# State products interleaved with the softmax denominators, and a list schedule built again from traced durations

## The chip, the cores and the metric

The kernel runs on one core of one Trainium2 chip. The metric is the device time of one execution in microseconds (us); smaller is better. A core has five engines with a queue each: TensorE (PE in the profile; its weight loads are the row PEld), VectorE (DVE), ScalarE (ACT), GpSimd (POOL) and SyncE (SP), which here issues every DMA. The engines meet only through semaphores.

## The reference

One pre-norm transformer block over 2048 tokens of width 1024, in bf16. The attention has 32 heads of width 32 and works on four segments `s` of 512 tokens; each head carries a state `M` (32x32) and a sum of keys `z` from segment to segment. Then a gated feed-forward block of width 3584 (FFN). Cut to what matters:

```python
phi = lambda t: jnp.where(t > 0, t + 1.0, jnp.exp(t))
...
for s in range(N):                       # 4 segments, 32 heads
    p = softmax(einsum('bhqd,bhkd->bhqk', qs, ks) * scale + mask)
    a_dot = einsum('bhqk,bhkd->bhqd', p, vs)
    a_mem = einsum('bhld,bhde->bhle', phi(qs), M) / (einsum('bhld,bhd->bhl', phi(qs), z)[..., None] + 1e-06)
    outs.append(g * a_mem + (1.0 - g) * a_dot)
    M = M + einsum('bhld,bhle->bhde', phi(ks), vs)
    z = z + einsum('bhld->bhd', phi(ks))
...
h = x + attention(layernorm(x)) @ wo
h2 = h + (silu(layernorm(h) @ w1) * (layernorm(h) @ w3)) @ w2
```

## The kernel before, in words

**Recording and planning.** The program is not written in the order in which it runs. Methods of `Kernel` record operations in a `Graph`: each operation has an engine (or a choice of two), a cost in ns, the regions that it reads and writes, a class and a sequence number. `Graph.schedule` then plays a list scheduler: at each moment an engine takes the ready operation with the lowest class and number. What comes out is one fixed order for each engine, which `Graph.emit` writes down with semaphore waits. Costs are the planner's alone: they decide the order and, between DVE, ACT and POOL, who does a copy; they are not in the program. DMAs are operations of SP; their landing is planned from `DMA_RATE`, `DMA_FIX` and a byte count that `scale` corrects. Each call of `stage()` begins a numbered unit, and the table `SHIFT` gives a unit an offset of its sequence number and of its class: it is the knob with which the order was searched. `LATER` moves single units of PE's final order by hand.

**Work on TensorE.** Three kinds of matmuls share it. *Full* ones (128x128 weights, up to 512 columns, line L759): projections, output projection, FFN. *Score* bursts (L1113, 32-row tiles): four or eight matmuls that fill PSUM banks 0 to 3, which ACT empties with one exponential over 128x2048 (L1127); there are ten for each half of the heads of each segment, 80 in all. *Column* bursts (128x32 tiles): for every segment and half, four numerators (L1206, `et` times `v`), the denominators (L1206, `et` and partial sums against `ones32`, one piece for each of the four heads `j`) and, for `s` below 3, the state products (L1041): 64 matmuls of 33 columns that add up `phi(k)^T [v, 1]` in PSUM bank 7. Besides, six *retrieval* bursts (L1328). Full matmuls have banks 5, 6 and 7 while attention lasts, and all eight afterwards.

**Order around the change.** `finish` records numerators 0 to 2, the denominators, numerator 3 and then, by `memory`, the 64 state products as one operation of PE. The denominators already hold both banks (`Both(gd, gm)`: 4 and 7). Behind them DVE transposes the denominators (L1237), takes reciprocals, and adds the state products to `Macc` (L1056, L1057), which gives bank 7 back. The FFN's first half is started while attention still runs, to fill PE between score bursts. A full matmul waits until its bank has been emptied by a copy (DVE L783 or ACT L782) or, in the FFN, by tanh (ACT L1401) and two products (DVE L1404, L1409). Layer norm of later tiles (DVE L886 on `xs`) waits for loads from DRAM.

Of the kernel before, what the change touches and what calls it, by code (L numbers as in the profile page):

```python
# [30 lines left out]
    0: (-18, 0), 3: (-173, 0), 4: (-182, 0), 5: (1074, 0), 6: (1041, 1), 7: (-959, -1),  # L31
    8: (-283, 1), 9: (1560, 1), 10: (-14, 0), 11: (1, 0), 12: (51, -1), 13: (-257, 0),
    14: (-1703, 0), 15: (2952, 0), 16: (-2912, 0), 18: (-87, -1), 19: (3455, 1), 20: (-401, -1),
    21: (22, 0), 22: (2924, -1), 23: (-669, 0), 24: (-328, -1), 26: (-261, -1), 27: (11, -1),
    28: (-153, 0), 29: (-317, 0), 31: (1524, -1), 32: (211, 0), 33: (-1, 0), 34: (2, 0),
    35: (-15, 0), 38: (118, 1), 39: (2057, 0), 40: (223, 0), 41: (2279, -1), 42: (914, 1),
    43: (-1135, 1), 44: (2665, 1), 45: (3218, 1), 47: (1997, 1), 48: (664, -1), 49: (1928, -1),
    50: (-2800, -1), 51: (7, 0), 52: (-1130, 0), 53: (116, 0), 54: (669, 0), 55: (1018, 0),
    56: (2, 0), 57: (-289, 1), 58: (4, 0), 59: (731, 0), 60: (-304, 0), 61: (-436, 0),
    62: (64, 1), 63: (-3, 0), 64: (-63, 0), 65: (-50, 0), 66: (-174, 0), 67: (-937, 0),  # L40
    68: (808, 0), 69: (1512, -1), 70: (28, 0), 71: (-58, 1), 72: (1441, 1), 73: (-75, 1),
    74: (2141, 0), 75: (778, 1), 76: (-752, 1), 77: (90, 1), 78: (-21, 0), 79: (151, 0),
    80: (1343, 0), 81: (-1130, 0), 83: (160, 0), 84: (687, 0), 85: (-676, 0), 86: (312, 0),
    87: (-266, 0), 88: (-263, 0), 89: (-1189, -1), 90: (-164, 0), 91: (680, 1), 92: (-1801, 0),
    93: (1499, 0), 94: (3153, 0), 95: (-261, 0), 96: (0, -1), 97: (-11, 0), 98: (2, 0),
    99: (944, 0), 100: (-54, 0), 101: (1016, 0), 102: (-842, 0), 103: (147, 0), 104: (-1191, 0),
    106: (-47, 0), 107: (121, 1), 108: (-1142, 0), 109: (-1295, -1), 111: (699, 0),
    112: (-365, -1), 113: (-594, 0), 115: (28, 0), 116: (2452, -1), 117: (-8, 0), 118: (676, 0),
    119: (54, 0), 120: (-1449, -1), 121: (235, 0), 122: (-9, -1), 123: (-13, 1), 124: (45, 0),
    125: (-1279, 1), 127: (-283, -1), 129: (555, 0), 130: (1438, -1), 132: (617, 1),  # L50
    133: (81, 0), 134: (-2285, -1), 135: (-179, 0), 136: (3199, 1), 137: (389, 0),
    138: (920, 0), 139: (146, 1), 140: (687, 1), 141: (27, 0), 142: (-619, 1), 143: (1934, 1),
    144: (-922, 0), 145: (415, -1), 146: (-312, 0), 147: (-26, 0), 148: (-870, 0),
    149: (2501, 1), 150: (1682, 0), 151: (-28, 0), 152: (609, 1), 153: (611, 0), 154: (-302, 0),
    156: (0, 1), 157: (-185, 1), 158: (391, 0), 159: (-373, 0), 160: (-610, 0), 161: (-1748, 0),
    162: (-133, 0), 163: (-4056, 1), 164: (1073, 1), 166: (-202, 0), 168: (-3204, -1),
    169: (-2075, -1), 170: (2581, -1), 171: (-39, 1), 172: (-122, 1), 173: (-18, 1),
    174: (-37, 0), 175: (34, 0), 176: (1853, 1), 177: (-140, 0), 178: (-301, 0), 179: (204, 0),
    181: (165, 0), 182: (-13, 0), 183: (-7, 0), 184: (687, -1), 185: (-271, 0), 186: (-861, 1),
    187: (-616, 1), 188: (355, -1), 189: (-1449, 1), 190: (1132, 0), 191: (114, 0),  # L60
    192: (-22, 0), 193: (-464, 0), 194: (-2, 0), 195: (294, 0), 196: (18, 0), 197: (-2089, 0),
    199: (-2443, 0), 200: (248, -1), 201: (1, 0), 203: (210, 1), 204: (-1070, 0), 206: (-70, 0),
    207: (1441, 0), 208: (525, 0), 209: (839, 0), 210: (10, 0), 211: (-262, 0), 212: (894, -1),
    213: (203, 1), 214: (-359, 1), 215: (-2, 0), 216: (696, -1), 217: (-735, 0), 218: (-51, 0),
    219: (4750, 0), 220: (-465, -1), 221: (-23, 0), 222: (-196, 1), 223: (399, 0),
    224: (-1932, 1), 225: (-192, 0), 226: (-134, 0), 227: (-1542, 1), 229: (153, 1),
    230: (-676, 1), 231: (-73, 0), 232: (618, 1), 234: (-465, 0), 235: (0, -1), 237: (222, -1),
    238: (609, 0), 239: (1282, 0), 241: (-183, 1), 242: (845, 1), 243: (811, -1),
    244: (1681, -1), 246: (6, 1), 248: (-2423, -1), 249: (11, 0), 250: (21, 0), 251: (-2902, 1),
    252: (-599, 1), 253: (927, 0), 255: (308, -1), 256: (4, -1), 257: (-382, 0), 258: (30, 0),  # L70
    259: (-35, 0), 260: (-73, -1), 261: (-386, 0), 262: (-58, 1), 263: (-1713, 0),
    264: (-165, 0), 265: (-369, 1), 266: (-12, 0), 267: (808, -1), 268: (1356, 0),
    269: (-538, 0), 270: (576, -1), 272: (27, 0), 273: (609, 0), 275: (-27, 0), 277: (0, -1),
    279: (-4, 0), 280: (-3, 0), 281: (176, 0), 282: (-28, -1), 284: (-175, -1),
    285: (-1255, -1), 286: (-196, 0), 287: (308, 0), 288: (1028, 0), 289: (-18, 0),
    290: (-217, -1), 291: (628, 0), 292: (21, 0), 293: (11, 0), 294: (1042, 0), 295: (6, 0),
    296: (150, -1), 297: (222, 0), 298: (1329, 0), 299: (-799, 0), 300: (-3, 0), 301: (303, -1),
    302: (-473, -1), 303: (2419, -1), 304: (528, 0), 305: (-99, 0), 306: (2531, -1),
    307: (-28, 0), 309: (-1338, 1), 310: (-4, 1), 311: (836, 0), 312: (-154, 0), 315: (-261, 0),
    316: (443, 0), 317: (-31, -1), 318: (-1464, -1), 319: (-220, 0), 320: (340, 0),  # L80
    321: (1268, 0), 322: (-21, -1), 323: (-2755, 1), 324: (-54, 0), 325: (1643, -1),
    326: (-57, 0), 327: (1851, 0), 328: (-2912, 0), 329: (317, 1), 330: (-690, 0),
    331: (-712, -1), 332: (-940, 0), 333: (-1099, 1), 334: (-615, 1), 335: (-16, 0),
    336: (496, 0), 337: (664, 0), 338: (-166, 0), 339: (-46, 0), 340: (-700, 0), 341: (-385, 1),
    342: (-1713, 0), 344: (51, 0), 345: (-756, -1), 346: (178, -1), 348: (803, 0),
    350: (1942, -1), 351: (169, 0), 352: (-492, 1), 354: (14, 0), 355: (-39, 0), 356: (290, 0),
    357: (99, 0), 358: (-389, 0), 359: (1761, 0), 361: (1409, 0), 362: (-58, -1), 363: (550, 1),
    364: (-95, 1), 365: (-140, 1), 366: (56, 1), 367: (-11, 1), 368: (-1627, 0),
    369: (-393, -1), 370: (-2089, 0), 372: (27, 0), 373: (204, -1), 374: (-55, 0),
    375: (-622, 0), 376: (-1005, -1), 377: (-179, 0), 378: (-1188, 1), 379: (1478, -1),  # L90
    380: (-865, -1), 381: (-543, 0), 382: (-70, 0), 383: (-64, 0), 384: (-1160, 0),
    385: (-2800, 0), 386: (0, 1), 387: (-193, 1), 388: (-133, 0), 390: (2419, 0),
    391: (2201, -1), 392: (-35, -1), 394: (45, -1), 395: (-2041, 0), 396: (410, 0),
    397: (571, 1), 399: (-543, -1), 400: (-965, 0), 401: (2531, 0), 402: (-462, -1),
    403: (-129, 0), 404: (-89, 1), 405: (-60, -1), 407: (-887, 1), 408: (3072, 0),
    409: (3013, 0), 410: (1761, 1), 411: (1584, 0), 413: (281, 1), 414: (562, 0),
    415: (-1293, -1), 416: (1707, 0), 417: (-995, -1), 418: (1637, 0), 419: (-785, -1),
    420: (3, 0), 422: (-913, -1), 423: (-121, -1), 424: (-7, 0), 426: (-2, 0), 427: (-1, 0),
    430: (-1, 0), 431: (14, 0), 432: (8, 0), 433: (-33, 0), 435: (-1086, 0), 436: (72, 0),
    437: (51, -1), 438: (-293, -1), 439: (37, 1), 440: (1527, 1), 441: (-212, 0),  # L100
    442: (-3190, 1), 443: (-1357, -1), 444: (-520, 1), 445: (904, 0), 446: (-1018, -1),
    447: (697, 0), 449: (2458, 0), 450: (-40, 0), 451: (-44, 0), 452: (-8, 0), 453: (-14, 0),
    454: (658, -1), 455: (-3, 0), 456: (1, 0), 457: (-3, 0), 459: (-2315, 1), 461: (-1, 0),
    462: (539, 0), 463: (66, 0), 464: (788, 1), 465: (29, 0), 466: (24, 0), 467: (2995, 0),
    468: (-306, 1), 469: (310, 0), 470: (-30, -1), 471: (-796, 0), 472: (-70, 1),
    473: (3455, 1), 474: (62, -1), 475: (-550, 0), 476: (-2089, 0), 477: (2158, 0),
    478: (-306, 1), 479: (4, 0), 480: (1506, -1), 481: (-470, -1), 482: (3857, 0),
# [21 lines left out]
}  # L129


LATER = {362: 2}


class Op:
# [54 lines left out]
class Graph:  # L190
# [7 lines left out]
    DMA_FIX = 1900.0  # L198
# [120 lines left out]
    def dma(self, out, in_, cls=5, deps=(), scale=1.0):  # L319
        n = 1  # L320
        for s in out.shape:
            n *= s
        o = self.op("sp", 60.0, None, reads=(in_,), writes=(out,), cls=cls, deps=deps,
                    kind="dma")
# [16 lines left out]
    def schedule(self):  # L341
# [24 lines left out]
        now = 0.0  # L366
# [1156 lines left out]
```

## Time and profile before

| what | value |
|---|---|
| three runs | 887.76, 889.54, 890.42 us; median 889.54 |
| profiled execution | span 887.6 us from the first to the last instruction; its time with what lies around the span is not listed |
| granted TensorE clock | 1.000 |
| PE busy | 872.2 us, 98% of the span, 5732 matmuls recorded |
| DVE, ACT, POOL busy | 449.0, 302.8 and 177.9 us |
| state products L1041 | 384 matmuls recorded, 176/184/191 ns each (shortest, median, longest), overlapping |
| DMA | 105.75 MB, mean 119 GB/s |

How to read it: matmuls are pipelined, so a busy row of PE says that some matmul was in flight, not that it streamed at full rate. What a matmul costs is the step from its start to the next one's start: 0.216 us for 512 columns. A full matmul that is started later than that after the one before stood still for something, also where the busy row shows no gap. A few per cent of the matmul records are missing, so a step of two or three times 0.216 us can be a missing record.

Attention and the work that is mixed into it take the first 376 us; then PE runs FFN alone.

### The profile page before, as it was taken

Reading aid. Unit: us, or ns where it says so; the run is one execution under the profiler, and the core shown is the slowest. Engines: PE = TensorE matmul, PEld = TensorE weight load, DVE = VectorE, ACT = ScalarE, POOL = GpSimd, SP = SyncE. Lnnn points to the kernel's source line nnn. Section 1 sums busy time; section 2 is a strip of 40 time slices with the busy share of each in tenths; the row PEclk is TensorE's granted clock in tenths of the full one; section 3 lists DMA queues with packets and bytes.
Section 4 is the critical chain, followed back from the end, with each engine's and each line's share of the span. In section 5 each row is a group of like instructions: output and inputs, shape, how many; then the busy total and the mean of one; then the engine's idle time right before and its main releaser. Section 6 shows DMA issues by size and latency. Waiting matters only on the chain.

```text
span 887.6 us, 13648 instructions
## 1 busy us (share of the span) xinstructions
PE 872.2 (98%) x5732; PEld 399.9 (45%) x5821; DVE 449.0 (51%) x699; ACT 302.8 (34%) x345; POOL 177.9 (20%) x226
## 2 busy tenths in 40 slices
PE   8999999999999999999999999999999999999998
PEld 5443444444444344444444444444444444444445
DVE  5697888787665697645545401323233333341011
ACT  5877675778645565611111000101011111110000
POOL 2544444445352455303000000000000000000000
PEclk9999999999999999999999999999999999999999
DMA  7869939464862737198454411221223321301110
GB/s 237 206 177 244 222 104 250 142 156 119 206 162 67 184 67 172 50 294 256 113 153 109 115 41 30 73 69 54 79 61 93 95 72 48 90 7 41 30 54 24
DMA packets 148796, 105.75 MB, mean 119 GB/s; under 512 B 46336, under 2 KB 134400, under 8 KB 147712
## 3 DMA queue, kind: packets, MB, share of 16 engines
q1 hardware_dynamic: 148736, 104.89, 44.5%
q8 instruction: 46, 0.75, 0.3%
q14 instruction: 14, 0.11, 0.0%
HBM read 84.94 MB, written 9.44 MB: 106 GB/s over the span
## 4 chain that ended last, share of the span: by engine, by line
PE 95%; DVE 1%; DMA 1%; SPq 1%; issue 1%; ACT 0%; POOL 0%; DVEq 0%; ACTq 0%
PE ps L759 89%; PE ps L1206 3%; PE ps L1113 3%; DMA xs<-in_A_x_dram 1%; SPq L325 1%; PE ps L1041 0%; DVE lnst L886 0%; PE ps L1328 0%; DVE R L1341 0%; ACT et L1127 0%; POOL et L1136 0%; DVE hm L1409 0%; PE ps L1199 0%; DVE t L1404 0%; ACT sg L1401 0%
## 5 line engine op out<-in xcount | busy, mean ns | idle before, releaser
L759 PE MATMUL ps<-hnT,w1b 128*128 128x512 bf16 x874 | 219.6, 379 | 1.9 <-issue 0.7
L759 PE MATMUL ps<-hnT,w3b 128*128 128x512 bf16 x880 | 217.3, 379 | 2.3 <-DVE t L1404 0.9
L759 PE MATMUL ps<-w2b,hm 128*128 128x512 bf16 (+2 forms) x935 | 198.5, 366 | 0.9
L1401 ACT ACTIVATE sg<-ps 128x512 bf16<-128x512 f32 x112 | 66.8, 597 | 384.9 <-PE ps L759 382.8
L1404 DVE SCALAR_TENSOR_TENSOR t<-sg,ps 128x512 bf16<-128x512 bf16 x112 | 76.7, 684 | 182.0 <-ACT sg L1401 181.6
L1127 ACT ACTIVATE et<-ps 128x2048 bf16<-128x2048 f32 x80 | 149.9, 1874 | 46.3 <-PE ps L1113 45.9
L759 PEld LDWEIGHTS ps<-w2b,hm 128*128 128x128 bf16 x952 | 90.9, 98 | 103.0
L759 PEld LDWEIGHTS ps<-hnT,w3b 128*128 128x128 bf16 x896 | 86.3, 98 | 107.0 <-issue 4.9
L759 PEld LDWEIGHTS ps<-hnT,w1b 128*128 128x128 bf16 x896 | 86.1, 98 | 106.3 <-issue 6.5
L1136 POOL TENSOR_SCALAR_AFFINE_SELECT et<-et 128x512 bf16<-128x512 bf16 (+1 forms) x96 | 92.8, 974 | 133.5 <-ACT et L1127 133.3
L1409 DVE SCALAR_TENSOR_TENSOR hm<-t,ps 128x512 bf16<-128x512 bf16 x112 | 76.1, 684 | 40.9 <-PE ps L759 39.0
L1433 DVE TENSOR_TENSOR ob<-hr,ps 128x512 bf16<-128x512 bf16 (+2 forms) x34 | 22.2, 655 | 120.6 <-PE ps L759 120.4
L759 PE MATMUL ps<-xnT,wp 128*128 128x512 bf16 (+1 forms) x345 | 59.8, 320 | 2.6 <-DVE kT L783 1.0
L759 PE MATMUL ps<-wo,oT 128*128 128x512 bf16 x246 | 60.9, 379 | 1.1 <-issue 0.8
L759 PE MATMUL ps<-hnT,wp 128*128 128x512 bf16 x249 | 59.5, 380 | 0.8 <-issue 0.6
L1150 DVE TENSOR_TENSOR sum<-sum,et 128x512 bf16<-128x512 bf16 (+1 forms) x64 | 43.0, 675 | 11.0 <-ACT et L1127 5.6
L759 PEld LDWEIGHTS ps<-xnT,wp 128*128 128x128 bf16 x352 | 27.9, 98 | 28.4 <-issue 2.8
L759 PEld LDWEIGHTS ps<-wo,oT 128*128 128x128 bf16 x256 | 23.9, 98 | 30.0 <-issue 3.3
L759 PEld LDWEIGHTS ps<-hnT,wp 128*128 128x128 bf16 x256 | 23.4, 98 | 30.0 <-issue 3.9
L1113 PE MATMUL ps<-qT,kT 32*128 32x128 bf16 (+3 forms) x512 | 31.7, 301 | 0.0
L759 PE MATMUL ps<-wp,xnT 128*128 128x512 bf16 x123 | 30.2, 379 | 0.4 <-issue 0.2
L759 PE MATMUL ps<-wp,hnT 128*128 128x512 bf16 x123 | 29.6, 380 | 0.5 <-issue 0.3
(97 smaller groups left out, 558.8 us busy)
## 6 DMA issues: line engine op xcount, KB each, us to landing
w3b<-in_B_w_dram SPq DMA_DIRECT2D x28, 512.0 KB, 4.0
w1b<-in_B_w_dram SPq DMA_DIRECT2D x28, 512.0 KB, 4.0
wp<-in_A_wv_dram SPq DMA_DIRECT2D x8, 1024.0 KB, 6.6
wp<-in_A_wq_dram SPq DMA_DIRECT2D x7, 1024.0 KB, 5.5
wp<-in_A_wk_dram SPq DMA_DIRECT2D x7, 1024.0 KB, 7.6
w2b<-in_B_w_dram SPq DMA_DIRECT2D x7, 1024.0 KB, 5.5
xs<-in_A_x_dram SPq DMA_DIRECT2D x16, 256.0 KB, 6.3
h<-in_A_x_dram SPq DMA_DIRECT2D x16, 256.0 KB, 3.8
```

Of the source, the lines that this page charges most:

```text
L325: o.emit = lambda e, g: [e.dma_start(out, in_)]
L759: return [e.matmul(p[0](gr), p[1], p[2], start=p[3], stop=p[4]) for p in part]
L1113: ins.append(e.matmul(self.bank(gr, j, 512 - 128 * kc, off), k[r, g0 + g, 128 * kc:128 * kc + 128], q[r, g0 + g, 128 * kc:512], start=True ...
L1127: return [e.activation(et[:, :, :], src, AF.Exp, scale=self.scale)]
L1136: self.pool_op(lambda e, v=v, pat=pat: e.affine_select(v, v, pattern=pat, compare_op=ALU.is_ge, fill=0.0, base=0, channel_multiplier=-1), ...
L1150: lambda e, gr: [e.tensor_tensor(out, x, y, op=ALU.add)], reads=[x, y],
L1206: ins.append(e.matmul(self.ps[32 * i:32 * i + 32, b * 512 + c0:b * 512 + c0 + n], lhsT(i, kc, j), rhs(i, j), start=kc == 0 and j == first, ...
L1401: self.g.op("act", act_ns(512), lambda e, gr, sg=sg: [e.activation(sg, self.bank(gr), AF.Tanh, scale=0.5)], writes=[sg], cls=0, group=gg)
L1404: e.scalar_tensor_tensor(t1, sg, 1.0, self.bank(gr), op0=ALU.add, op1=ALU.mult)], reads=[sg], writes=[t1], cls=0,
L1409: e.scalar_tensor_tensor(dst, t1, 0.5, self.bank(gr), op0=ALU.mult, op1=ALU.mult)], reads=[t1], writes=[dst], cls=0,
L1433: self.g.op("dve", dve_ns(n), lambda e, gr, hs=hs, ob=ob, n=n: [e.tensor_tensor(ob, hs, self.bank(gr, 0, n), op=ALU.add)], reads=[hs], wri ...
```

## The change

1. `memory` records no matmuls any more. The 64 state products are emitted by a new function `products` inside the denominators' operation: after the twelve denominator matmuls of head `j` come the sixteen products of head group `i = j`. The denominators' cost for the planner grows by 4 x 80 ns where the burst has cost 16 x 42 ns by itself.
2. The planner's constants: the DMA fixed time from 1900 to 1560 ns, SP's time for an issue from 60 to 400 ns (420 for the row copies, 1250 for a transposing DMA), byte scales for most loads, and a begin at 800 ns.
3. Groups of the output projection, of FFN up and of FFN down may claim a PSUM bank only after the group before them of the same kind (`after`).
4. `SHIFT` is another table, and `LATER` is empty. All engine orders change with it.

```diff
-LATER = {362: 2}
+LATER = {}
...
-    DMA_FIX = 1900.0
+    DMA_FIX = 1560.0
+    BEGIN = 800.0
...
-        o = self.op("sp", 60.0, None, reads=(in_,), writes=(out,), cls=cls, deps=deps,
+        o = self.op("sp", 400.0, None, reads=(in_,), writes=(out,), cls=cls, deps=deps,
...
-        o = self.op("sp", 60.0, None, reads=(in_,), writes=(out,), cls=cls, kind="dma")
+        o = self.op("sp", 1250.0, None, reads=(in_,), writes=(out,), cls=cls, kind="dma")
...
-        o.bytes = 2 * 262144
+        o.bytes = 130000
...
-        now = 0.0
+        now = self.BEGIN
...
-    def dense_group(self, late=False):
+    def dense_group(self, late=False, after=()):
...
-        o = self.g.op("pe", 16 * 42.0, emit, reads=[pkn[:, :, :], v[:, :, g0:g0 + 4, :, :]], cls=1,
-                      group=gr)
-        o.mode = "col"
...
+        def products(e, b, i):
+
+            pkn = self.pkn
+            return [e.matmul(self.ps[32 * j:32 * j + 32, b + 33 * i:b + 33 * i + 33],
+                             pkn[:, 4 * i + kc, 32 * j:32 * j + 32], v[:, kc, g0 + i, j, 0:33],
+                             start=kc == 0, stop=kc == 3, tile_position=(0, 32 * j),
+                             skip_group_check=True) for kc in range(4) for j in range(4)]
...
+                    if isinstance(gr, Both):
+                        ins += products(e, gr.parts[1].banks[0] * 512, j)
...
+            if isinstance(gr, Both):
+                cost += 4 * 80.0
...
-                   None if s else 0, [self.ones32[:, :, :]] + ([self.pkn[:, :, :]] if gm else []),
+                   None if s else 0, [self.ones32[:, :, :]] + ([self.pkn[:, :, :], v[:, :, g0:g0 + 4, :, :]] if gm else []),
...
-                gr = self.dense_group(s >= 2)
+                gr = self.dense_group(s >= 2, self.outs[-1:])
+                self.outs.append(gr)
...
-                gg, gu = self.dense_group(True), self.dense_group(True)
+                gg, gu = self.dense_group(True, self.ups[-1:]), self.dense_group(True)
+                gu.after = frozenset((gg,))
+                self.ups.append(gu)
```

## The prediction

> **What bounds the kernel now.** I read the page's shares first, then the chain of work that ended last, then the chain in order of time, and last PE's instructions one by one around every late start.
>
> ```profile
> span 887.6 us, 13648 instructions
> PE 872.2 (98%) x5732; PEld 399.9 (45%) x5821; DVE 449.0 (51%) x699; ACT 302.8 (34%) x345; POOL 177.9 (20%) x226
> ...
> PE   8999999999999999999999999999999999999998
> DVE  5697888787665697645545401323233333341011
> ACT  5877675778645565611111000101011111110000
> ...
> PE 95%; DVE 1%; DMA 1%; SPq 1%; issue 1%; ACT 0%; POOL 0%; DVEq 0%; ACTq 0%
> ```
>
> PE is the bound everywhere and 95% of the chain is PE itself. DVE and ACT are busy to 80 or 90% only in the first 17 slices (the 376 us of attention); there alone can a planner's order cost anything. Behind 376 us the chain in order of time shows 49 full matmuls in 10.79 us, piece after piece, which is the bare 0.216 us step plus a missing record: nothing to gain there but one late start of 0.15 us at 459 us.
>
> So the change can move three things: what the state products cost PE, PE's late starts in the first 376 us, and new late starts.
>
> **Part 1, the products.** PE's order of time around one burst (start, duration, line, count):
>
> ```profile
> 95.64 0.23 PE L1206 MATMUL ps<-et,ones 128*32 128x128 bf16 x4
> 95.70 0.72 PE L1206 MATMUL ps<-et,v 128*32 128x512 bf16 x16
> 96.24 0.69 PE L1041 MATMUL ps<-v,pkn 128*32 128x33 bf16 x64
> 97.09 0.38 PE L759 MATMUL ps<-wp,hnT 128*128 128x512 bf16 x1 [0.16 <-issue]
> ```
>
> The 64 products sit between the last numerator and full work. One by one, their quads (four column tiles, which start together) begin 25 ns apart for the first seven, and then, after one step of 59, some 33 ns apart, each of the 64 about 8.3 ns behind the last. So the burst outruns the supply of instructions after 28 matmuls. First to last start takes 510 to 512 ns in five bursts; the sixth (179.8 us) takes 737, with one hole of 250 where 25 to 33 is usual. A block of sixteen is shorter than the 28 that run fast, and between two blocks stand twelve denominators, which take 273 ns for 24 instructions and let the supply catch up. So I price a block at four quads of 25 to 28 ns, 104 ns, and four blocks at 415. The old burst, with its own entry of 46 ns and exit, costs 520: 0.105 us less for each of six bursts, 0.63 in all, and 0.23 for the hole, which no short block should meet: **-0.86 us**. The ends: no gain if the sixteen run at 33 ns (4 x 4 x 33 = 528), and 6 x (520 - 4 x 4 x 14) = 1.8 us if they streamed at the denominators' own rate of 53 ns for 128 columns, 14 for 33. I take 25, since that is the same instruction's own row.
>
> The Trainium skill, TensorE: Matmul & The Clock Gate, section "Wait — 56ns, not 53.3ns?", says that start-to-start never falls below about 25 ns however few columns. It speaks against the 1.8: by it the products save no more than the 0.6 above. The row of 25 ns agrees.
>
> Nothing else of part 1 is on the path. The tile shape (128*32) is that of the denominators, and the whole order has 80 score, 8 column and 6 retrieval bursts before and after, so the changes of tile shape (0.312 us into a burst and 0.317 out of it, instead of 0.216 each) stay 94. `v` is a new read of the denominators, but three numerators that read it stand ahead on the same queue. The DVE transpose of the denominators (L1237) comes up to 0.4 us later; its followers feed the retrieval one attention later. Bank 7 comes back up to 0.5 us earlier where the burst stood behind numerator 3. If the transpose were urgent it would cost 8 x 0.4 us at the very most.
>
> **Part 2, the late starts.** Against steps of 0.216, they are, from 17 us on: 1.19 us at 20.9, 0.18 at 76, 0.33 at 176 (numerators wait for POOL's mask), 0.13 at 259, 0.16 at 267 (tanh), 1.04, 0.31 and 0.18 at 303, 305 and 310 (DVE behind a retrieval), 0.15 at 459: **3.67 us**. This is all that a better order could win, and the largest is typical of what a planner with wrong times does:
>
> ```profile
> 20.04 1.04 PE L759 MATMUL ps<-xnT,wp 128*128 128x512 bf16 x4
> 22.10 1.90 PE L759 MATMUL ps<-xnT,wp 128*128 128x512 bf16 x8 [1.03 <-DVE kT L783]
> ...
> 18.98 2.47 DVE L886 BATCH_NORM_STATS2 lnst<-xs 128x6 f32<-128x512 bf16 x4 [2.84 <-DMA xs<-in_A_x_dram]
> 21.37 0.67 DVE L783 CAST kT<-ps 128x512 bf16<-128x512 f32 x1
> ```
>
> PE's four matmuls end their steps at 20.90 and the next wait for a copy of `kT` that stands on DVE behind four layer-norm statistics, which waited 2.84 us for a load that lands at 18.96. In the changed order that `kT` copy is on ACT (copies of `kT` on ACT go from 15 to 20), and DVE's next copy behind the statistics is one of `qT`. By hand, with DVE's rows (0.65 a statistic, 0.7 a sum, 0.5 an apply), sixteen operations from 18.98 on put that copy near 28.3; PE asks for its bank some 84 matmuls behind the first score burst, near 33. So **-1.19**.
>
> What comes in its place in the same stretch: (a) ACT. From the first exponential at about 19.0 it does exponentials of 1.88 and copies of 0.5 to 0.6; the copy of `qT` stands ahead of the fourth exponential and waits for PE to 29.1, so that exponential ends near 31.6, where PE wants the banks at about 30.7: up to 0.9 us. (b) The first `wk` load of the second half can be issued near 24.2, when PE has read the buffer. The `wq` load of the same size took 5.5 us (25.33 to 30.85), so it lands at 29.7, more with the two transposing DMAs behind it on SP; its first reader is 68 instructions behind the first burst, at about 29.8: 0 to 2 us. I take +0.7 for both together.
>
> The other holes hold 2.48 us. I can't walk through all of that order, but two counts speak for fewer holes. A score cycle of twelve full matmuls takes PE 12 x 0.216 + 0.41 = 3.0 us; ACT has 1.78 for the exponential, start to start, 0.5 for each copy and 0.95 for a phi exponential. Before, 14 of 80 cycles hold more ACT work than PE work, 3.7 us too much in sum; after, 9 with 2.6. And DVE gives seven product or copy operations net of its load to POOL and two to ACT; behind the fourth retrieval (the 1.04) PE has 32 full matmuls before the next score burst instead of 16, so DVE's four L1341 (0.74 each) have double the time. I take half: **-1.24**, between 0 and -2.48.
>
> The first 17 us (2.4 us of late starts, most for the first tile, landed 3.4, the first `wq`, 7.7, and the fourth tile, 8.4) stay: the first nine loads are issued in the same order, and the fourth tile's chain (ACT sums, POOL, DVE apply at 12.2) still sets the end. PE then has the same matmuls left; by hand the same work is done at 18.5 instead of 18.4: +0.1.
>
> `after` and `LATER` add no instruction; FFN groups from 376 us on have eight banks and 3.45 us for each pair, against 0.6 on ACT and 1.4 on DVE. Weight loads there (4.0 us a half, 13.8 us ahead) stay hidden. If that cover went, each would cost its lateness.
>
> **Sum.** -0.86 - 1.19 + 0.7 - 1.24 + 0.1 = -2.5 us. The profiled span of 887.6 becomes 885.1. The median of the runs stands 1.9 above the span; I keep that distance: 889.5 - 2.5 = **887.0 us**. A measurement of this kernel tells 0.3% (2.7 us) from no change, so the forecast lies just inside "within".
>
> **Rivals.**
> 1. The order wins nothing: new holes are as large as the old ones, only the products' gain is left: 888.7. For it: what the plan cannot know (DVE slowed to 1.70 us for a product, twice its 0.7, while POOL works at 306 us) is as before.
> 2. The order is nearly free of holes: -0.86 - 3.67 and half of (a) and (b), 0.4: 885.4. For it: 2.4 of the 3.67 us sit at two places, and both are rearranged.
> 3. Slower, by one mechanism: weight loads that come late because SP stands in front of them. SP is in order, and a transposing DMA held its queue 2.25 us (29.21 to 31.46) and 2.42 (32.27 to 34.69) where the new plan charges 1.25. Loads now stand directly behind such DMAs in attention, as in (b). Each load late by 1.5 us stops PE 1.5 us, since no other full work is allowed past it. Against gains of 2.5 it takes two to break even and four to be 3.5 us slower: 893.0. Against it: before, with the coarser prices of 60 ns, only one such late start (0.5 us at 7.8) was there.
> 4. The change doesn't do what it says: products stay at 33 ns in blocks. That adds 0.9 to the forecast, 887.9, within its range.
>
> **Chances.** Forecast with its near range (885.8 to 888.4, the fourth rival in it) 0.50, first rival 0.16, second 0.15, third 0.19. Faster by over 0.3% means below 886.9: the second rival and a little over half of the forecast, 0.42. Slower by over 0.3% (above 892.2) takes two thirds of the third rival and what I may have missed in the stretches not walked: 0.18. Within: 0.40. The range reaches from the second rival to short of the third's end, 884.6 to 891.8.
>
> **What would show it.** Right: blocks of sixteen products with quads 25 to 28 ns apart and no hole, six times about 0.1 us; no wait of PE on `kT` behind L886 near 20 us; late starts between 17 and 376 us that sum to about 2 us; 10.79 us for 49 matmuls behind it, with the last score burst and the end of attention at the same place. Wrong: quads at 33 ns or more; a wait of PE for `wp` loads near 30 us or later; ACT as the releaser of score bursts again and again; any holes behind 376 us, which would mean that the claims in order (`after`) hold banks back.

## The result, and the profile after

| | before | after |
|---|---|---|
| median (runs) | 889.48 us (4) | 898.49 us (4) |
| ratio, 95% interval | | 1.0099 [1.0086, 1.0113] |
| span of the profiled execution | 887.6 us | 897.5 us |

The change costs 9 us. The forecast was 887.0 us, and its range ended at 891.8. The granted TensorE clock is 1.000 in both profiled executions. The page of the changed kernel: the span, busy time, then PE, DVE and ACT in tenths by slice, then the shares of the chain that ended last.

```profile
span 897.5 us, 13708 instructions
...
PE 872.9 (97%) x5733; PEld 398.7 (44%) x5821; DVE 440.6 (49%) x690; ACT 303.5 (34%) x347; POOL 186.5 (21%) x233
...
PE   8989899999999999999999999999999999999998
...
DVE  5777768777566676747562132113333343323111
ACT  6857685767746464611110010001111111101000
...
PE 88%; DMA 7%; DVE 1%; issue 1%; SPq 1%; ACT 1%; POOL 0%; DVEq 0%; ACTq 0%
```

PE's own work is the same (872.9 against 872.2 us). What is new stands in the last line: DMA holds 7% of the chain where it held 1%. The chain in order of time (start, length, what) says which ones:

```profile
30.37 5.69 DMA wp<-in_A_wq_dram
44.09 6.77 DMA wp<-in_A_wv_dram
56.87 6.32 DMA hnT<-xs
...
104.70 6.53 DMA wp<-in_A_wk_dram
...
185.19 1.45 issue
...
246.20 12.90 DMA R<-r_scr
...
298.88 11.19 DMA R<-r_scr
```

And PE's waits (total, times, longest):

```profile
...
PE ps L760 <- DMA wp<-in_A_wk_dram: 3.4, 2, 2.0
PE ps L760 <- DMA wp<-in_A_wv_dram: 2.7, 3, 1.0
PE ps L760 <- DMA hnT<-xs: 1.5, 1, 1.5
PE ps L1197 <- issue: 1.4, 1, 1.4
PE ps L1323 <- DMA R<-r_scr: 1.2, 2, 0.9
...
PE ps L760 <- DMA wp<-in_A_wq_dram: 1.2, 2, 1.0
```

Measured as in the prediction, by the step to the next start, PE's late starts from 17 us on sum to 13.6 us, all of them before 387 us, against 3.9 before with the hole in the sixth burst. 10.1 of the 13.6 end with a DMA's landing: weights 0.34 at 35 us, 0.96 at 50, 1.04 at 100, 2.15 at 109, 1.14 at 239, 1.54 at 247; the transposing DMA into `hnT` 1.52 at 61; the `R1` copies 0.37 at 259 and 1.01 at 309. A copy of `qT` on DVE accounts for 0.7 (70 us), two holes that no semaphore explains for 2.3 (185 and 230 us, see the last section), the rest is 0.4. The first full-width matmul comes at 17.85 instead of 16.36 us, and the products give some 0.65 back: 9.7 + 1.5 - 0.65 = 10.5, which is 0.6 more than the 9.9 between the spans; that difference is not accounted for. Behind attention PE again takes 10.79 us for 49 matmuls.

The largest of these holes, first on SP's queue and then on PE:

```profile
102.17 2.48 SPq L332 DMA_TRANSPOSE pkn<-pk  x1
104.70 0.58 SPq L325 DMA_DIRECT2D wp<-in_A_wk_dram  x1
105.32 2.62 SPq L332 DMA_TRANSPOSE xnT<-xs  x1
107.99 0.59 SPq L325 DMA_DIRECT2D wp<-in_A_wq_dram  x1
```

```profile
108.25 1.03 PE L760 MATMUL ps<-wo,oT 128*128 128x512 bf16 x4
111.27 1.04 PE L760 MATMUL ps<-hnT,wp 128*128 128x512 bf16 x4 [1.99 <-DMA wp<-in_A_wk_dram]
```

SP stands 2.5 us in each transposing DMA, the load between them lands 6.5 us after its issue, and PE waits for it. It looks as if SP's order did it; the experiments say otherwise.

### The profile page after: what moved, and what is told of

The parts are those of the page before. It is cut to its first block, busy times and chain, and to the rows that moved or that the text cites. A ratio compares the mean times of both kernels' runs of the same rounds, so it can differ in the third digit from the quotient of the medians.

```text
span 897.5 us, 13708 instructions
## 1 busy us (share of the span) xinstructions
PE 872.9 (97%) x5733; PEld 398.7 (44%) x5821; DVE 440.6 (49%) x690; ACT 303.5 (34%) x347; POOL 186.5 (21%) x233
## 4 chain that ended last, share of the span: by engine, by line
PE 88%; DMA 7%; DVE 1%; issue 1%; SPq 1%; ACT 1%; POOL 0%; DVEq 0%; ACTq 0%
PE ps L760 82%; PE ps L1197 3%; DMA R<-r_scr 3%; PE ps L1096 2%; DMA wp<-in_A_wq_dram 1%; DMA wp<-in_A_wv_dram 1%; SPq L1288 1%; DMA wp<-in_A_wk_dram 1%; DMA hnT<-xs 1%; DMA r_scr<-T 1%; ACT et L1110 0%; SPq L332 0%; PE ps L1178 0%; DVE oT L1303 0%; PE ps L1323 0%
## 5 line engine op out<-in xcount | busy, mean ns | idle before, releaser
L760 PE MATMUL ps<-hnT,w1b 128*128 128x512 bf16 x876 | 225.1, 379 | 2.0 <-issue 1.3
L760 PE MATMUL ps<-hnT,w3b 128*128 128x512 bf16 x878 | 225.3, 379 | 1.1 <-issue 0.2
L1119 POOL TENSOR_SCALAR_AFFINE_SELECT et<-et 128x512 bf16<-128x512 bf16 x96 | 92.8, 973 | 130.7 <-ACT et L1110 129.2
L1339 POOL TENSOR_TENSOR oT<-Nsb,R 128x512 bf16<-128x512 f32 x22 | 30.0, 1381 | 8.3 <-DVE lnmv L890 5.7
```

What stands on the lines that cost most here:

```text
L760: return [e.matmul(p[0](gr), p[1], p[2], start=p[3], stop=p[4]) for p in part]
L1119: self.pool_op(lambda e, v=v, pat=pat: e.affine_select(v, v, pattern=pat, compare_op=ALU.is_ge, fill=0.0, base=0, channel_multiplier=-1), ...
L1339: self.either(lambda e, out=out, Ns=Ns, R1=R1: e.tensor_tensor(out, Ns, R1, op=ALU.add), 512, 2, [Ns, R1], [out], 2)
```

## The experiments

**Theory.** The planner's new DMA prices leave no room. Where DMAs queue up, the time from the landing of the DMA before to its own is, as the median in the changed kernel's trace, about 0.9 us for a transposing DMA of 256 KB (0.8 to 1.0 by kind and by which of them one counts as queued; 0.9 to 1.0 in before's), 3.0 for 1 MB of weights, 1.2 for a row copy. The old plan charged 2.02, 4.03 and 1.01 us of the queue; the new one 0.50 (130000 bytes at 260 per ns), 3.51 and 1.20. So a transposing DMA went from 1.1 us too dear to 0.4 too cheap; there are forty. Against that, the 21 weight loads of 1 MB behind the start stay 0.5 us too dear each. **Rivals:** the spread products cost; the new order of DVE and ACT; the order of single DMAs on SP; a search that fitted shifts to its plan, whatever the prices.

### The products alone

```diff
 # before: memory's 64 matmuls leave their place; in each head's denominators:
+                    if isinstance(gr, Both):
+                        ins += products(e, gr.parts[1].banks[0] * 512, j)
```

> The kernel before with its own order, SHIFT, LATER and prices; only the products of the six bursts are issued sixteen behind each head's denominator, as in the changed kernel. Against before (889.5 us). Theory (the loss comes from when the DMAs land, the products themselves gain what the denominators' rows show): 6 bursts x 4 heads x about 28 ns, so 0.6 to 0.9 us faster, 888.6 to 888.9 us, and the late starts of PE those of before. Rival (the products cost in their new place, by a hole of PE's instruction supply or by the moved wait on the values): 889.5 us or more. Rival (the loss is all of the new order and prices, nothing of the products): says the same as the theory here.

Ratio 0.9991 [0.9982, 1.0000], 0.8 us faster: the products gain about what their rows promised, though the interval just reaches no change. The changed kernel's blocks, one after the other:

```profile
94.46 0.23 PE L1197 MATMUL ps<-et,ones 128*32 128x128 bf16 x4
94.52 0.26 PE L1178 MATMUL ps<-v,pkn 128*32 128x33 bf16 x16
94.62 0.28 PE L1197 MATMUL ps<-et,ones 128*32 128x256 bf16 x4
```

From 94.52 to 94.62 us: sixteen products in about 0.10 us, so 0.41 us for the four blocks of a burst, where the old block of 64 took 0.52.

> The changed kernel with its order and prices; in each of the six bursts the sixty-four products of the four heads stand in one block behind the denominators of the fourth head instead of sixteen behind each head. Theory: the bursts give back the 0.6 to 0.7 us that the spread won, so 0.3 to 0.9 us slower than the changed kernel, about 899 us. Rival (the spread products are what costs 9 us): 890 us or less.

Here the products of all four heads stand behind the loop over heads. 1.0117 [1.0097, 1.0137], 1.5 us above the changed kernel by the medians against before, but the intervals overlap; the profiled span is 897.0 us. The size is not settled; that the spread products would cost 9 us is excluded.

### What lands late

```diff
-                self.g.dma(w[:, :, :], src, cls=1, scale=0.87)
+                o = self.g.dma(w[:, :, :], src, cls=1, scale=0.87)
+                o.emit = lambda e, g, w=w, src=src: [e.dma_start(w[:, 0:4, :], src[:, 0:4, :])]
```

> The changed kernel with its order; each weight load of q, k and v behind those of the start brings only row chunks 0 to 3 of the eight (half the bytes), so half of those weights is left out and the matmuls, which are the same in number and size, read what the tile held before. Theory (weights and hidden-state transposes land late because the plan prices the DMAs too tightly): the holes behind the weight loads go, those at 35, 50, 109, 239 and 247 us of 0.3, 1.0, 2.2, 1.1 and 1.5 us, and the transposes at 61 us land sooner too; 6 to 9 us off, 889 to 893 us. Rival (the new order of the work of ACT and DVE is what holds PE, the loads are only where it shows): less than 2 us off, 896 us or more.

889.41 us, ratio to before 0.9999 [0.9984, 1.0013]: all of the loss is gone with 11 MB of traffic, and DVE's and ACT's order is the same. In the profiled execution (891.67 us) one wait grew, 2.5 us for a `wk` load at 238 us; the other waits for weights sum to 0.4 us and that for `hnT` is gone. So the order of DVE and ACT is not the cause.

```diff
-        o.emit = lambda e, g: [e.dma_start_transpose(out, in_)]
+        o.emit = lambda e, g: [e.dma_start(out, in_.rearrange("p (c t) -> p c t", c=8))]
```

> The changed kernel with its order; each of the forty transposing DMAs (xs into hnT and xnT, hn into hnT, pk into pkn) is a plain DMA of the same 256 KB in the same place, so the transposition is left out and what is computed behind it is another thing of the same size. Theory, sharpened: the transposing DMAs, priced at 0.5 us of transfer and 1.25 us of SP, are what makes everything behind them on SP and its queues late, since they take up to 4.1 us of SP and land 0.7 to 1.1 us apart; without them the weight loads stand less long behind SP and the holes at 50, 61, 109, 239 and 247 us shrink: 3 to 8 us off, 890 to 896 us. Rival (the 1 MB weight loads themselves, at 6 to 7.5 us to landing where 5.5 are planned, are what is late, the transposes only stand beside them): less than 2 us off, 896.5 us or more.

900.19 us, 1.0112 [1.0093, 1.0131]: the theory's sharpened form missed. A plain copy holds SP for 0.6 us when nothing is queued (the transposing one 1.24) and for 2.5 to 4.0 us in four places; all forty take 37.5 us of SP, the transposing ones 84.7. But its step in the queue is 0.66 (`pkn`) to 1.6 us (`xnT`), in the mean about 0.9 as for the transposing one, and the `wk` load of 105 us lands 8.6 us after its issue instead of 6.5. So neither the transposition nor SP's time for it makes the loss: what SP saves, the loads wait in the queue.

```diff
+        if key in self.filled or out.tensor.name == self.xn:
+            out, in_ = out[:, 0:4, :], in_[:, 0:512]
```

> The changed kernel with its order; of the forty transposing DMAs those whose destination has been written before (10 of the 12 of pk, the second filling of the hidden-state tiles and the last of xnT, 22 in all) bring only half of their 256 KB, so half of these transposes is left out and the matmuls read older contents there. A step of them should then take about the 0.5 us that the plan charges. Theory (the under-priced transposes are the main part of the lateness): those that stand in front of the wk load at 105 us and of the loads at 235 to 247 us get cheaper; 1.5 to 5 us off the changed kernel, 893.5 to 897 us. Rival (the weight loads alone, their price of 5.5 us against 6 to 7.5, make it late; the transposes are a side show): less than 1 us off.

896.28 us, 1.0078 [1.0059, 1.0097], 2 us off by the medians, but the intervals overlap: a half takes 0.50 to 0.55 us of the queue, which is the plan's price, and the holes of 109 and 239 us fell to 1.25 and 0.88, that of 247 us went, while that of 35 us grew from 0.34 to 1.02. The time lies in the theory's band, without being clear of noise.

### The order of single DMAs

> The changed kernel, with the four copies of R1 for the numerators issued by SP ahead of the four of R0w wherever they stand behind them (the four plus four of each half where both are rebuilt). Theory (PE waits for the R1 copies at 259 and 309 us because SP and the queues bring R0w's first): those holes of 0.4 and 1.0 us shrink or go, up to 1.4 us faster than the changed kernel, 897 us, less what later R0w copies then cost. Rival (the copies are late because their source is, not because of the order): same within 0.3 us.

```diff
-R0w R0w R0w R0w R1 R1 R1 R1
+R1 R1 R1 R1 R0w R0w R0w R0w
```

913.06 us, 1.026 [1.0242, 1.0278]: 15 us slower than the changed kernel. The premise was wrong. The copies land one every 1.2 us, so the last of `R0w` came at 258.6 instead of 254.5 us, and what DVE does with them holds the PSUM banks for which PE then waited:

```profile
PE ps L770 <- DVE kT L794: 4.3, 1, 4.3
PE ps L770 <- DVE hm L1418: 4.2, 2, 3.7
```

Part of the 15 us is not waiting: at these two waits the granted clock is at half for 6.8 us each, which costs at least 4.1 us in 19 full matmuls (see the last section).

> The changed kernel with one exchange in SP's order: the wk load that SP issued at 104.70 us goes ahead of the pk transpose in front of it, whose issue began at 102.17 us. Theory (a load comes late because SP stands in front of it, the third rival of the prediction): wk is issued 2.5 us earlier, the hole of 2.15 us at 108.9 us goes for the most part; 1.0 to 2.3 us off the changed kernel, 896.2 to 897.5 us. Rival (the queue behind SP is full, whoever is issued first): the load lands no earlier and the time is that of the changed kernel within 0.5 us.

What ran was another exchange: the `wq` load of 107.99 us went ahead of the `xnT` transpose, because the rule asked for a buffer that was free by the plan. 898.19 us, 1.0093 [1.0078, 1.0108]: no change. It says nothing of `wk`, but this `wq` load, issued 2.7 us earlier, landed only 1.2 us earlier (113.97 instead of 115.12 us). The exchange that was meant:

> The changed kernel with the exchange that was meant before: the wk load issued at 104.70 us goes ahead of the pk transpose that SP began at 102.17 us (the earlier run exchanged the wq load behind it with an xs transpose instead, since the plan had wk's buffer free only after the transpose's start). Theory (the load is late because SP and the queue serve the transpose first): wk lands 1.5 to 2.5 us earlier and the hole of 2.15 us at 108.9 us goes for the most part; 1 to 2.2 us off the changed kernel, 896.3 to 897.5 us. Rival (the queue is full anyway, or what is pushed back stops PE instead): within 0.5 us of the changed kernel.

900.77 us, 1.0135 [1.0115, 1.0155]: not faster, and by the intervals 2 to 3 us slower than the changed kernel, which its profile, of the fastest of four executions (898.66 us), doesn't explain. In its trace:

```profile
110.43 1.04 PE L766 MATMUL ps<-hnT,wp 128*128 128x512 bf16 x4 [0.98 <-DMA wp<-in_A_wk_dram]
...
116.30 1.04 PE L766 MATMUL ps<-hnT,wp 128*128 128x512 bf16 x4 [1.48 <-DMA wp<-in_A_wq_dram]
```

The wait for `wk` halved, from 1.99 to 0.98 us, and a wait of 1.48 for the next load, `wq`, took its place. `wk` was issued 2.4 us earlier and landed 0.8 us earlier. Here the exchange only chose who waits.

> The kernel before with the products spread as in the first experiment, and in SP's order each write of the denominators' state (T to r_scr) that stood behind loads of w1 and w3 goes ahead of them: three places, of which the one at 288 us matters, where the write waited behind 1 MB and took 4.5 us to land. Theory (these are the DMAs whose landing stops PE at 304 and 311 us): the write lands about 2 us earlier, the R and R0w copies too, and of the two holes of 0.9 us each 1.0 to 1.8 us goes; 2 to 2.7 us faster than before, 887 to 887.7 us. Rival (another wait takes their place, the w1 and w3 loads that now come later): within 0.5 us of the first experiment, 888.5 us or more.

900.65 us, 1.0121 [1.0106, 1.0136]: the edit did more than was meant. It also carried the two loads of 265 us behind the write at 288 us, and PE wanted them at 285:

```profile
PE ps L779 <- DMA w1b<-in_B_w_dram: 9.2, 1, 9.2
```

> As the experiment with the state's write ahead of the loads, but only the write at 288 us goes ahead, and only past the two loads of w1 and w3 issued at 285 us, not past the pair of 265 us, which PE needs at 285 us. Theory: the write lands about 2 us earlier and so do the copies; of the holes of 0.9 us each at 304 and 311 us 1.0 to 1.8 us goes; 1.9 to 2.7 us faster than before, 887 to 887.9 us. Rival (w1 and w3, now later, or another wait take their place): within 0.5 us of the first experiment, 888.5 us or more.

889.94 us, 1.0007 [0.9996, 1.0017]: not faster than the products alone. The write landed 2.3 us after its issue instead of 4.5, but the copies behind it still queued behind the same two loads (the last `R0w` landed 16.9 us after the write's issue instead of 17.8). The hole of 304 us stayed at 1.04 us and that of 310 went. Against it, this run's profile has a wait of 1.1 us for a `wq` load at 128 us that the first experiment's lacks, though nothing was changed there; so the 0.9 us may be real and is not shown.

### How much room each order has

```diff
+        for o, src, to in self.flat:              # flat: every transposing DMA
+            t = Op(("sp",), o.cost, lambda e, g, src=src, to=to: [e.dma_start(to, src)], 0, 0)
...
+            order["sp"].insert(order["sp"].index(o) + 1, t)
```

> The kernel before with its order; behind each of the forty transposing DMAs SP issues a plain DMA of the same source, 256 KB, to a DRAM scratch that nobody reads (added work: 10 MB; nothing waits for it but whoever overwrites the source). Theory (its planner priced a transposing DMA at 2.0 us of the queue where the trace shows steps of 0.9 us, so its list has room for about 1 us more at each): 0 to 3 us slower than before, 889.5 to 892.5 us. Rival (the room is not in the prices; an order with such a load would suffer as much as the changed kernel does): 8 us slower or more, 897.5 us and up.

> The changed kernel with its order and the same forty extra DMAs of 256 KB to a scratch. Theory (its prices, 0.5 us for a transposing DMA that takes 0.9, left no room): every one of them pushes what follows; 8 to 25 us slower than the changed kernel, 906 to 923 us, and several times what the same copies cost the kernel before. Rival (the order is late for another reason than DMA room): the same addition as in the kernel before, within 2 us.

The same 10 MB: before goes to 891.80 us, 1.0029 [1.0016, 1.0042]; the changed kernel to 911.43, 1.0244 [1.0219, 1.0269]. That is +0.3% for one order and +1.4% (1.0244 against 1.0099), 13 us, for the other. Of the 13 us, 2.8 to 5.1 are the clock, which was at half for 10.2 us in all, at two waits of 4.2 us; it was not below 1.00 in the other profile. The copies also hold their sources, so that whoever overwrites one can wait for them. PE's waits for DMAs in the one (first fence) and in the other:

```profile
PE ps L770 <- DMA wp<-in_A_wq_dram: 1.1, 2, 0.9
...
PE ps L770 <- DMA h<-in_A_x_dram: 0.4, 1, 0.4
```

```profile
PE ps L771 <- DMA wp<-in_A_wv_dram: 6.0, 3, 4.2
PE ps L771 <- DMA wp<-in_A_wk_dram: 4.8, 2, 4.2
PE ps L771 <- DMA wp<-in_A_wq_dram: 2.3, 2, 1.4
...
PE ps L771 <- DMA hnT<-xs: 1.7, 1, 1.7
```

### Prices or search

The planner computes its own end of its list when the program is built: 885.1 us for after, whose span is 897.5. For before the author gives 888.7 (span 887.6), a figure that no run here keeps.

> The kernel before with its prices, without any of its SHIFT and LATER: the list as the costs alone make it; the planner's own end of that list is 914.1 us. Theory (the old prices of the DMAs leave a margin, whatever the shifts): the span comes out at the planner's end or below it, 911 to 915 us. Rival (a plan holds only where shifts were chosen by what the chip did): 920 us or more.

> The changed kernel with its new prices, without any of its SHIFT: the list as the new prices alone make it; the planner's own end of that list is 917.1 us. Theory (the new prices are too low, so any list that they make comes out late): a span 5 to 14 us over the planner's end, 922 to 931 us. Rival (the prices are right on the whole, and the 12 us between the plan of the changed kernel, 885.1, and its span of 897.5 come from shifts fitted to the plan): within 3 us of the plan, 914 to 920 us.

Spans 919.5 and 930.2 us, of one execution each: 5.4 and 13.1 over their plans. The second is in the theory's band. The first is in neither: 7.6 us of its waits are on the `R` copies, which the old prices charge 0.2 us too little each. The plan doesn't know the clock either, which was at half for 20.5 us in the first (4.5 to 10.2 us lost) and for 30.7 us in the second (6.3 to 15.4). So the 7.7 us more in the second are lateness and its echo in the clock; these two runs can't tell how much is which.

So three lists from one and the same search, with the changed kernel's code:

```diff
-        o.bytes = 130000        # both: another SHIFT
+        o.bytes = 2 * 262144    # only in the second
```

> The changed kernel with its prices and another SHIFT: some 1500 trials of a plain search from the empty list, kept when the planner's own end fell (917.1 to 893.9 us). Theory (the price of the transposing DMA, 0.5 us of the queue where the trace shows 0.9, makes any list late): the span is 7 to 14 us over the plan, 901 to 908 us. Rival (the miss belongs to the one list on record): within 4 us of the plan, 892 to 898 us.

> The same code, prices and search with one price changed: a transposing DMA charged 2.0 us of the queue, as before's planner did; the planner's end went from 921.2 to 898.4 us in as many trials. Theory: the room that this leaves takes up the lateness; a span within 3 us of the plan, 896 to 901.5 us, and shorter than that of the list with the cheap price although its plan is 4.5 us longer. Rival (this price does not matter): as far over its plan as the other list, and so longer than it, 905 us or more.

> The same code and search with all prices of before's planner; its end went from 915.3 to 900.4 us. Theory: within 4 us of the plan, 898 to 905 us; it charges the R copies 1.0 us where the trace shows 1.2 us, so it may stand a little further over its plan than the list with the dear transposes alone. Rival (prices don't matter): 7 to 14 us over its plan, 907 us or more.

| list | plan | span | over | median, ratio |
|---|---|---|---|---|
| new prices | 893.9 | 903.4 | +9.5 | 906.02, 1.0189 [1.0159, 1.0219] |
| new prices, transposing DMA at 2.0 us | 898.4 | 896.5 | -1.9 | 900.03, 1.0122 [1.0072, 1.0172] |
| all old prices | 900.4 | 899.9 | -0.5 | 901.58, 1.0139 [1.0110, 1.0169] |

```profile
span 903.4 us, 13708 instructions
```

```profile
span 896.5 us, 13706 instructions
```

All three stand against their plans as the theory said. The plan that looks 4.5 us worse gives a span 6.9 us shorter, by one constant (6.0 us by the medians, of two runs each, whose intervals just overlap). Of the 6.9, some 2 are the clock (at half for 6.8 us in the first list, 3.4 in the second, with 3.0 and 0.9 us lost in full matmuls). So lateness is not a matter of the list on record alone, and it goes with that price: three lists with the cheap transposing DMA come out 9.5 to 13.1 us over their plans, three with the dear one 1.9 under to 5.4 over. But there is one searched list for each set of prices, and a search can hit a better or worse one by chance; how many of the 9 us this one price makes is not shown. (None of the three lists is near before's; 1500 trials are few.)

## Why the prediction was wrong

**Part 1** held: quads start 25 to 28 ns apart, as priced, -0.63 for the blocks came out at about -0.65, and the kernel with the products alone measures -0.8 us. (The 25 ns are from quad to quad; inside a quad the four matmuls start 3 to 4 ns apart. Sixteen steps of 25 ns would have allowed 0.72, not only the 0.6 of the prediction.) Its second term failed: "0.23 for the hole, which no short block should meet". The hole went elsewhere; with the products alone it stands between numerators at 179.5 us, with 0.64 us, and in the changed kernel there are two, 1.7 and 0.6 us.

**-1.19 for the `kT` copy** held, partly by luck: there is no late start near 21 us, but four other executions of before's own order, with the products alone, the state's write moved (two runs) and the extra copies, show 0.2 to 0.9 us there. The 1.19 was the largest of five, not a constant of the order. **(a) and (b), +0.7**: the `wk` load took 5.65 us as foreseen; PE did not wait for it, but 0.34 us for the `wq` load behind it. The mechanism was right and the size within its bounds.

**"The first 17 us stay ... +0.1"** was too small: +1.5 us at the first full-width matmul. The nine loads are issued in the same order; their landings differ from run to run by some tenths (the first `wq` 7.5 to 8.5 us). Orders like before's begin full-width work at 16.4 to 16.8 us in these runs, orders like after's at 16.9 to 17.9; the two profiles compared here are the earliest of the one kind and the latest of the other, so some of the 1.5 us is chance.

**"I take half: -1.24, between 0 and -2.48"** is the step that failed. The other holes did not shrink; they grew from 2.5 us to 13, and 10 of these end with a DMA's landing. The two counts behind it were on ACT's and DVE's work; no one counted the DMA queue. The trace of before had what was needed: steps of about 0.9 us or more for each transposing DMA against 0.50 in the new plan, forty of them, some 17 us of queue time that the plan does not know of, 34 of the forty in the first 400 us. The Trainium skill, DMA: Bandwidth & Descriptors, section "Latency and other measured facts", gives a transposing DMA with a non-contiguous middle dimension 261 GB/s. By that 256 KB take an estimated 1.00 us; the trace's 0.9 us are about 290 GB/s, near that, and the plan's 0.50 would be 524.

**The third rival** was what happened, at two and a half times its price (9 us against 3.5) and with half of its mechanism. Loads do come late, in six places and not four, with 0.3 to 2.2 us each; `hnT` and the `R1` copies too. But not "because SP stands in front of them": with plain copies SP spends less than half the time on them and nothing is won, and an exchange in SP's order wins nothing (898.19 and 900.77 us in the two that tried it). The argument against this rival, that before with coarser prices had only one such late start, was turned the wrong way: coarse in SP's 60 ns, but dear by 1.1 us in the transfer of each transposing DMA. Its order has room for more DMA work, and the changed kernel's has little, as the extra copies show (2 us for the one, 13 for the other).

## What to carry to other kernels

In a list schedule a price is also a margin. Here prices that were too high gave way to traced ones, and one that was now too low began to show; so compare every planned landing with the traced one, for the queues as well as for the engines, and leave the shared queue dearer than it is. When a new plan promises less time, ask which constant the promise comes from, and run the same order with more load on that resource: the order with room hardly moves. And look at the granted clock of every run before adding up its waits.

The version that comes out ahead is before's own order with the products spread, 0.9991 [0.9982, 1.0000], an interval that just reaches no change.

## What was not expected of the hardware

**A long wait of PE is paid twice.** In ten of the nineteen profiles the granted TensorE clock falls to half for 3.4, 6.8 or 10.2 us, in or just behind waits of PE, most of 2 us or more; in before and in the changed kernel it never does. In the list of the new prices, four full matmuls take 1.0 us behind a wait of 2.77, and the next twelve, eight of them at half the clock, take 4.4 instead of some 2.8. The last line is the stretch at half the clock (from and to, length, PE busy and matmuls, clock, DMA share, GB/s):

```profile
192.82 1.02 PE L741 MATMUL ps<-xnT,wp 128*128 128x512 bf16 x4 [2.77 <-issue]
...
194.11 4.44 PE L741 MATMUL ps<-xnT,wp 128*128 128x512 bf16 x12
```

```profile
194.14:197.50 3.36, 3.36 (x13) 0.50 1.71 254
```

The step is 0.427 us there instead of 0.216. A wait of 2.4 us for `hnT` (products in one block) brought no such stretch, so a wait of 2 us does not always bring one. Where the text gives a loss by the clock, the lower figure counts the full matmuls that took about 0.43 us, the upper is half of the time at half the clock.

**Holes that no semaphore explains.** The page counts 46 packets and 0.75 MB on queue q8, "instruction", some 16 KB each. The largest hole, that of 185 us,

```profile
184.53 0.66 PE L1197 MATMUL ps<-et,v 128*32 128x512 bf16 x11
186.63 0.33 PE L1197 MATMUL ps<-et,v 128*32 128x256 bf16 x5 [1.45 <-issue]
```

comes at the end of a packet of that queue that took 1.70 us, where the usual one takes about 1.1 us; the hole is 1.71. In other runs the same place shows a packet of 2.01 us and a hole of 1.99 (extra copies), 1.38 and 0.96 (`wq` moved), 1.21 and 0.58 (one block), and before's packet of 1.04 a hole of 0.23. The pairs are not always so close: 2.29 and 1.62 (plain copies), 2.17 and 1.35 (`wk` moved), 0.93 and 0.64 (products alone), and the changed kernel's second hole, 0.63 at 230 us, follows a packet of 1.06. The Trainium skill, Runtime: NRT & Kernel Launch, section "Instruction fetch mechanics", has the 16 KiB blocks and calls the crossing mostly hidden; if these holes are such crossings, it is not hidden here. No run isolated it: that PE waits for its instructions in these bursts, and that data DMAs slow the packets, is argued from these pairs only.
